# Attention, experts and a gated FFN on one core: routing tables filled during the first pair of heads, one copy issued later, output scales computed beside the experts, the last queries of two heads normalized together

## The chip, the cores and the metric

The kernel runs on one core of one Trainium2 chip. The core has five engines with a program each: TensorE (PE, matmul and transpose; its weight loads stand as PEld), VectorE (DVE), ScalarE (ACT), GpSimd (POOL) and SyncE (SP, which here issues nearly all DMAs). Each works its instructions off in the order in which they were issued and meets the others only at semaphores. The metric is the device time of one execution in microseconds (us); smaller is better.

## The reference

Three stages follow one another.

1. Attention, for 4 batches of 8 heads, 1152 keys, head width 64. Queries are averaged in twos, so 576 queries are left per head: `attn = softmax(q_pool @ k.T / 8)`, `out = attn @ v`. The heads of a batch side by side are the rows `x` (2304 tokens of 512).
2. A mixture of 8 experts with one expert per token: `logits = x @ w_gate`, the expert is the largest logit, its softmax probability the weight: `out[mask] = gate_w * (relu(x[mask] @ w1[e]) @ w2[e])`.
3. A gated FFN: `(x @ w_a) * (x @ w_b) @ w_out`, with the three matrices given in float64.

## The kernel before

**Tiling of the attention.** The 32 heads are worked in 16 pairs (`NPAIR`), two neighbouring heads at a time. Values are held as a high and a low float16 part, so that a product takes up to three matmuls. Of the 576 queries of a head, 512 are four full blocks of 128; the last 64 of both heads share a fifth block: queries 512 to 575 of head 0 in rows 0 to 63, those of head 1 in rows 64 to 127. `spread(p)` (L312, ACT) makes two copies per pair, one in `qq` and one in `qlt`: it puts the last columns of each head in a block by itself, with zeros beside it, for the row maxima of the fifth block.

**Two passes over the scores.** The first finds each query's maximum: `a_units` (L319) issues matmuls into PSUM tile `sa` (two buffers) for two (block, third of the keys) parts, and DVE takes the maximum (`mx`, L338). `finish_max` (L343) turns the maxima into two more rows of the query side (`rl`, by a DMA transpose). The second pass goes in 21 units per pair, `n` counted over all 336: `scores(n)` (L370, PSUM tile `sp`, two buffers), two exponentials on ACT (`pt` in float32, L387, and `ph` in float16, L389), `p_low` (L404), which on POOL subtracts them (`pl`, L407), and four units later (`LAG`) `av(n)` (L409), which multiplies `ph` and `pl` with the values.

**The order of the work** is written out by hand in the loop over `n` (L960 to L1064), and that order holds on every engine. `a_ends` (L929) spreads the first pass of a pair over units of the pair before: the rest of pair 0 goes to units 0 to 5, all of pair 1 to units 6 to 15. Table `U` (L955) gives the unit `u` of a pair at which the other work is issued: for pair p+2 the splitting and transposing of keys (`prep_k`, `prep_k_low`, `trans_k`) and queries (`prep_q`, `prep_q_low`, `trans_q1`, `spread`), loads for pair p+3, and the finishing of pair p-1: `norm(p-1, 1)` at u = 4, `norm_tail` at 6, `turn` (transposes on TensorE, then ACT) at 7 and 10, `turn_low` at 9 and 11, `mag_x` at 12, `logits` at 13. For pair 1 there is no pair before to hide in, so its first preparations come at n = 0 and 1: at n = 1 `trans_k(1)`, `prep_q_low(1)`, `trans_q1(1)` and `spread(1)`, whose two ACT copies read what the two DMA transposes of `trans_q1(1)` write.

**`norm_tail(p)`** (L468) divides the fifth block by its sums. It does head 0 with three DVE instructions on rows 0 to 63 and head 1 with three on rows 64 to 127, whose result goes to tile `xtl`; a DMA then moves it to rows 0 to 63, beside head 0, in `xe`. In the last pair both heads' last queries lie in rows 0 to 63 and no DMA is needed.

**Routing.** After the fourth pair of a batch, generators (`scales`, `gate`, `out_scale`) are appended to `gates`, and `aside()` takes one step of them in every second unit. `out_scale(b)` (L614) makes the factor by which a token's row is multiplied at the very end: five small DVE instructions (a sum over `gex`, the exponentials of the logits, plus 1e-9, a reciprocal, times `am`, the row's scale, and a product), in two steps. For batches 0 to 2 it runs in the attention, for batch 3 after `route()` (L1091). `places()` (L1220) runs beside the experts, two steps per slot of 64 tokens, and uses the factor `osc` at L1264.

**Start.** Before the first load is used, POOL writes the identity (`ident`), index tables (`iota_*`, `koff`, `tok_base`) and `upper`, and DVE the tables `desc`, `tri`, `pad_id`, `out_id` and `upper16`, and shifts `iota_row2` and `tok_base`. All are for the transposes of `turn` and for the routing; the DVE instructions that depend on POOL's tables (L137 to L143, L218) stand in DVE's program ahead of, in the order in which they ran, the low parts of pair 0's keys (L272). The matmuls `warm` (L886) only keep TensorE busy.

Of the kernel before, what the change touches and what calls it, by code (L numbers as in the profile page):

```python
# [27 lines left out]
def attn_moe_kernel(  # L28
# [58 lines left out]
    ident = cst.tile([128, 128], F32, name="ident")  # L87
    make_identity(nc, ident)
    ones_col = cst.tile([128, 1], F32, name="ones_col")
# [4 lines left out]
    nc.vector.memset(ones16, 1.0)  # L94


    desc, desc_ = [cst.tile([128, NTB, E], F32, name=f"desc{i}") for i in range(2)]
    for i, d in enumerate((desc, desc_)):
        for e in range(E):
            nc.vector.memset(d[:, :, e : e + 1], float(E - e))  # L100
        nc.vector.memset(d[64:128, NTB - 1, :], -float(i))

    tri = cst.tile([128, E, E], F32, name="tri")
    nc.vector.memset(tri, 0.0)
    for e in range(1, E):
        nc.vector.memset(tri[:, e, 0:e], 1.0)
    iota_row = cst.tile([128, 128], F32, name="iota_row")
    nc.gpsimd.iota(iota_row, pattern=[[1, 128]], base=0, channel_multiplier=0, allow_small_or_imprecise_dtypes=True)

    iota_row2 = cst.tile([128, 2, TS], F32, name="iota_row2")  # L110
    nc.gpsimd.iota(iota_row2, pattern=[[0, 2], [1, TS]], base=0, channel_multiplier=0, allow_small_or_imprecise_dtypes=True)

    iota_slot = cst.tile([128, 2, NP], F32, name="iota_slot")
    nc.gpsimd.iota(
        iota_slot, pattern=[[1, 2], [2, NP]], base=0, channel_multiplier=0, allow_small_or_imprecise_dtypes=True
    )
    iota_tile = cst.tile([128, NT // 128], F32, name="iota_tile")
    nc.gpsimd.iota(
        iota_tile, pattern=[[1, NT // 128]], base=0, channel_multiplier=0, allow_small_or_imprecise_dtypes=True
    )  # L120
    iota_part = cst.tile([128, 1], F32, name="iota_part")
    nc.gpsimd.iota(iota_part, pattern=[[0, 1]], base=0, channel_multiplier=1, allow_small_or_imprecise_dtypes=True)

    koff = cst.tile([128, 3, E], F32, name="koff")
    nc.gpsimd.iota(koff, pattern=[[1, 3], [0, E]], base=0, channel_multiplier=0, allow_small_or_imprecise_dtypes=True)
    iota_e = cst.tile([128, E], F32, name="iota_e")
    nc.gpsimd.iota(iota_e, pattern=[[1, E]], base=0, channel_multiplier=0, allow_small_or_imprecise_dtypes=True)

    tok_base = cst.tile([128, B, NTB], F32, name="tok_base")
    for i in range(2):  # L130
        nc.gpsimd.iota(
            tok_base[:, 2 * i : 2 * i + 2], pattern=[[SQ, 2], [128, NTB]], base=i * 128 - PAD * (1 - i),
            channel_multiplier=1, allow_small_or_imprecise_dtypes=True,
        )

    pad_id = cst.tile([128, 1], F32, name="pad_id")
    nc.vector.tensor_scalar(out=pad_id, in0=iota_part, scalar1=float(TS), scalar2=-float(TS), op0=ALU.is_ge, op1=ALU.mult)  # L137
    nc.vector.tensor_tensor(out=pad_id, in0=pad_id, in1=iota_part, op=ALU.add)
    nc.vector.tensor_scalar(out=pad_id, in0=pad_id, scalar1=float(PAD), scalar2=None, op0=ALU.add)
    for t in (iota_row2, tok_base):  # L140
        nc.vector.tensor_scalar(out=t, in0=t, scalar1=R_OFF, scalar2=None, op0=ALU.subtract)
    out_id = cst.tile([128, 1], F32, name="out_id")
    nc.vector.tensor_scalar(out=out_id, in0=iota_part, scalar1=float(PAD), scalar2=None, op0=ALU.add)  # L143
    lpx = cst.tile([128, 9, 1], F32, name="lpx")
# [59 lines left out]
    for i in range(3):  # L204
# [7 lines left out]
    upper = at.tile([128, 128], F32, name="upper")  # L212
    nc.gpsimd.memset(upper, 1.0)
    nc.gpsimd.affine_select(
        out=upper, in_=upper, compare_op=ALU.is_gt, fill=0.0, base=0, pattern=[[1, 128]], channel_multiplier=-1
    )
    upper16 = at.tile([128, 128], F16, name="upper16")
    nc.vector.tensor_copy(upper16, upper)  # L218

# [228 lines left out]

    xtl = at.tile([128, D], F32, name="xtl")


# [16 lines left out]
    def norm_tail(p):  # L468
        b, h = bh(p)
        x = xe[b][0:64, 4, 64 * h : 64 * h + 128]  # L470
        for j in range(2):
            o = tail(p, j)
            ps = slice(o.base_partition(), o.base_partition() + 64)
            r = rec[ps, 4 + j]
            nc.vector.tensor_scalar(out=r, in0=o[:, D : D + 1], scalar1=VC * PX * 1e-9, scalar2=None, op0=ALU.add)
            nc.vector.reciprocal(r, r)
            y = xtl[64:128] if ps.start else x[:, D * j : D * j + D]
            nc.vector.tensor_scalar(out=y, in0=o[:, 0:D], scalar1=r, scalar2=None, op0=ALU.mult)
            if ps.start:
                nc.sync.dma_start(out=x[:, D : 2 * D], in_=y)  # L480

# [44 lines left out]

    p2 = {}


    def scales(b):  # L530
        am = p2[b] = ap2.tile([128, NTB, 1], F32, tag="am", name=f"am{b}")
# [12 lines left out]

    gsum = {}

    def gate(b):
# [5 lines left out]
        yield  # L553
        ex = gsum[b] = ap2.tile([128, NTB, E], F32, tag="gex", name=f"gex{b}")
        nc.scalar.activation(ex, sh, AF.Exp)
        o = oh[:, b]
# [53 lines left out]
        )  # L610
        yield


    def out_scale(b):  # L614
        gs = ap2.tile([128, NTB, 1], F32, tag="gs", name=f"gs{b}")
        nc.vector.tensor_reduce(out=gs, in_=gsum[b], axis=AX.X, op=ALU.add)
        nc.vector.tensor_scalar(out=gs, in0=gs, scalar1=1e-9, scalar2=None, op0=ALU.add)
        yield
        nc.vector.reciprocal(gs, gs)
        nc.vector.tensor_tensor(out=gs, in0=gs, in1=p2[b], op=ALU.mult)  # L620
        nc.vector.scalar_tensor_tensor(out=osc[:, b], in0=gs, scalar=OS, in1=gs, op0=ALU.mult, op1=ALU.mult)
        yield
# [251 lines left out]
    with tc.manual_schedule():  # L874
# [85 lines left out]
        for n in range(NPAIR * NU):  # L960
# [64 lines left out]
            if p:  # L1025
                if u == U["n1"]:
                    norm(p - 1, 1)
                if u == U["nt"]:
                    norm_tail(p - 1)
                if u in U["t"]:  # L1030
                    turn(p - 1, [0, 1, 2, 3] if u == U["t"][0] else [4])
                if u in U["tl"]:
                    turn_low(p - 1)
                if u == U["mg"]:
                    mag_x(p - 1)
                if u == U["lg"]:
                    logits(p - 1)
                if p % HP == HP - 1 and u == U["sx"]:
                    store_x(p // HP, 0, HP - 1)
                if p % HP == 0 and u == U["g"]:  # L1040
                    gates.extend(x(p // HP - 1) for x in (scales, gate, out_scale))
            for _ in range(ASIDE[u] if n > 9 else 0):
# [46 lines left out]
        for _ in routing:  # L1089
            pass  # L1090
        gates.append(out_scale(B - 1))  # L1091
        while gates:
            aside()
    at_ctx.close()
# [125 lines left out]
    def places():  # L1220
# [38 lines left out]
        yield  # L1259

        bv = mp.tile([128, NB, 2, NO], F32, name="obv")
        nc.vector.tensor_tensor(out=bv[:, :, 0], in0=bm, in1=vf.to_broadcast([128, NB, NO]), op=ALU.mult)
        yield
        nc.vector.tensor_tensor(  # L1264
            out=bv[:, :, 1], in0=bm, in1=osc.rearrange("p b i o -> p (b i) o").to_broadcast([128, NB, NO]), op=ALU.mult
        )
# [206 lines left out]
```

## Time and profile before

| | |
|---|---|
| three runs | 1302.93, 1309.43, 1310.91 us (median 1309.43) |
| profiled execution | 1305.76 us; its span in the trace 1304.1 us |
| PE busy | 1181.3 us (91% of the span), 17154 matmuls |
| DVE busy | 798.9 us (61%), 1546 instructions |
| ACT busy | 648.2 us (50%), 1325 |
| POOL busy | 525.3 us (40%), 471 |
| mean granted TensorE clock | 0.963 |
| pass over the scores and routing (attention) | 0 to about 565 us |
| experts | about 567 to 861 us |
| gated FFN | about 866 us to the end |

How to read it: the span counts from the first instruction of the trace. Busy shares are means over three stages with different limits, so every reading that follows is of a stretch. In a row of a timeline the bracket at the end, `[5.10 <-ACT ph L389]`, says that the engine stood idle for 5.10 us just before that instruction, and that what it waited for last was ACT's instruction at line 389, which writes `ph`. The granted clock is a share of TensorE's full speed, 2.4 GHz; 0.50 is the lower of its two levels, 1.2 GHz.

### The profile page before, as it was taken

To read this page: it belongs to the slowest core of one execution; us is meant where nothing else is said; L and a number is where in the kernel's file an instruction comes from. 1 tells how busy PE (TensorE), PEld (TensorE's weight loads), DVE (VectorE), ACT (ScalarE), POOL (GpSimd) and SP (SyncE) were. 2 spreads that over 40 slices of the span, in tenths; PEclk is the share of its full clock that TensorE was granted. 3 is DMA by queue.
4 is the path that set the end of the run, shared out by engine and by line. 5 is a ranking of instruction groups with operands and counts; after the bars stand their busy time and mean duration, and the time that the engine had idled before them with its cause. 6 is when DMAs were issued, how large, how long until landed. Compare 5 with 4: busy or idle time off the path is not lost. (4 is left out here: it accounts for less than half of the span.)

```text
span 1304.1 us, 41111 instructions
## 1 busy us (share of the span) xinstructions
PE 1181.3 (91%) x17154; PEld 823.2 (63%) x17154; DVE 798.9 (61%) x1546; ACT 648.2 (50%) x1325; POOL 525.3 (40%) x471
## 2 busy tenths in 40 slices
PE   7799999899889998578978998989999999999996
PEld 6466665566556655378878997964555555555553
DVE  5678788778878887855485557238577722222221
ACT  3578887788778877522473336225443311111111
POOL 4578887788878877613243322100000000000000
PEclk9899999999999999778989998999999999999998
DMA  7666775566646533244187227113222100000000
GB/s 173 121 136 152 147 180 148 106 139 142 121 93 156 121 74 108 71 168 156 48 315 260 89 78 253 49 31 104 81 83 96 33 1 1 25 25 25 25 17 33
DMA packets 170508, 136.46 MB, mean 105 GB/s; under 512 B 101072, under 2 KB 136400, under 8 KB 170256
## 3 DMA queue, kind: packets, MB, share of 16 engines
q1 hardware_dynamic: 167056, 122.74, 35.4%
q0 software_dynamic: 3200, 10.53, 2.4%
q8 instruction: 136, 2.23, 0.7%
q14 instruction: 116, 0.95, 0.2%
HBM read 94.96 MB, written 9.74 MB: 80 GB/s over the span
## 5 line engine op out<-in xcount | busy, mean ns | idle before, releaser
L407 POOL TENSOR_TENSOR pl<-pt,ph 128x512 f16<-128x512 f32 (+1 forms) x330 | 383.3, 1178 | 112.5 <-ACT ph L389 82.8
L387 ACT ACTIVATE pt<-sp 128x512 f32<-128x512 f32 (+1 forms) x336 | 197.5, 588 | 103.9 <-PE sp L380 96.4
L338 DVE TENSOR_REDUCE mx<-sa 128x2 f32<-128x768 f32 x224 | 206.2, 923 | 70.2 <-PE sa L333 67.5
L1383 PEld LDWEIGHTS <-wc 128*128 128x128 f16 x1728 | 169.5, 98 | 125.0 <-PEq L1345 4.7
L1383 PE MATMUL ab<-x2h,wc 128*128 128x384 f16 x1152 | 212.0, 327 | 4.6 <-PEq L1345 4.6
L429 PEld LDWEIGHTS <-ph 128*128 128x128 f16 (+1 forms) x2880 | 151.3, 101 | 75.8 <-issue 35.5
L1422 POOL DMA_INDIRECT out_dram<-ob,idxo x18 | 17.5, 973 | 444.6 <-DVE ob L1421 411.7
L389 ACT ACTIVATE ph<-sp 128x512 f16<-128x512 f32 (+1 forms) x331 | 195.1, 590 | 0.0
L333 PE MATMUL sa<-kst,qq 128*128 128x384 f16 x480 | 159.1, 332 | 29.1 <-DVE mx L338 25.3
L429 PE MATMUL av<-vv,ph 128*128 128x65 f16 (+2 forms) x2880 | 168.9, 196 | 0.3 <-DVE ph L402 0.3
L1393 DVE TENSOR_TENSOR gf<-ab,sa 128x384 f32<-128x384 f32 x72 | 40.1, 557 | 194.5 <-PE ab L1383 194.4
L333 PE MATMUL sa<-kst,qlt 128*128 128x384 f16 x480 | 158.7, 331 | 0.0
L429 PE MATMUL av<-vv,pl 128*128 128x65 f16 (+1 forms) x1440 | 156.4, 194 | 1.0 <-POOL pl L407 1.0
L1182 PEld LDWEIGHTS <-w2c 128*128 128x128 f16 x3840 | 128.5, 102 | 28.7 <-issue 21.6
L380 PE MATMUL sp<-rl,k2b 66*128 66x512 f16 (+1 forms) x576 | 136.8, 292 | 8.0 <-DMA rl<-qln 7.1
L377 PE MATMUL sp<-qq,kst 128*128 128x512 f16 (+1 forms) x576 | 136.0, 290 | 7.3 <-ACT ph L389 7.2
L1161 PE MATMUL hp<-xh,w1c 128*128 128x64 f16 x2560 | 125.1, 194 | 6.1 <-issue 1.4
L1161 PEld LDWEIGHTS <-w1c 128*128 128x128 f16 x3840 | 120.3, 99 | 10.3 <-DVE w1c L866 5.4
L429 PEld LDWEIGHTS <-pl 128*128 128x128 f16 (+1 forms) x1440 | 123.8, 102 | 1.2 <-POOL pl L407 1.1
L1182 PE MATMUL yp<-hh,w2c 128*128 128x64 f16 x2560 | 114.0, 199 | 8.3 <-issue 3.6
L1161 PE MATMUL hp<-xl,w1c 128*128 128x64 f16 x1280 | 121.4, 194 | 0.0
L1383 PE MATMUL ab<-x2l,wc 128*128 128x384 f16 x576 | 117.3, 326 | 0.0
(230 smaller groups left out, 1825.0 us busy)
## 6 DMA issues: line engine op xcount, KB each, us to landing
raw<-in_moe_w_dram SPq DMA_DIRECT2D x20, 1024.0 KB, 6.9
rbw<-in_moe_w_dram SPq DMA_DIRECT2D x20, 1024.0 KB, 7.4
kr<-in_k_dram SPq DMA_DIRECT2D x16, 576.0 KB, 5.2
vr<-in_v_dram SPq DMA_DIRECT2D x16, 576.0 KB, 6.1
qr<-in_q_dram SPq DMA_DIRECT2D x32, 256.0 KB, 3.5
cl<-in_moe_w_a_dram SPq DMA_DIRECT2D x12, 512.0 KB, 3.5
cl<-in_moe_w_b_dram SPq DMA_DIRECT2D x12, 512.0 KB, 3.7
cl<-in_moe_w_out_dram SPq DMA_DIRECT2D x12, 512.0 KB, 3.4
```

The source lines that it names most:

```text
L333: nc.tensor.matmul(sa[:, i, :KA], lhsT=x[:, 128 * b_ : 128 * b_ + 128], rhs=kst[:, j, ks], start=o == 0, stop=o == len(ops) - 1,)
L338: nc.vector.tensor_reduce(out=s["mx"].rearrange("p t n -> p (t n)")[:, ones[0] : ones[0] + m].rearrange("p (m o) -> p m o", o=1), in_=sa[: ...
L377: nc.tensor.matmul(sp[:, o : o + w], lhsT=s["kst"][:, j, ks], rhs=s["qq"][:, c0 : c0 + w], start=True, stop=False)
L380: nc.tensor.matmul(sp[:, o : o + w], lhsT=k2b[p % 3][:, j, ks], rhs=s["rl", j if w > 64 else 1][0:66, c0 : c0 + w], start=False, stop=True,)
L387: nc.scalar.activation(pt[:, :o], sp[:, :o], AF.Exp, scale=1.0 / (16.0 * SC * SC))
L389: nc.scalar.activation(phb[n % NPB][0][:, :o], sp[:, :o], AF.Exp, scale=1.0 / (16.0 * SC * SC))
L407: eng.tensor_tensor(out=l[:, :w], in0=pts.pop(n)[:, :w], in1=h[:, :w], op=ALU.subtract)
L429: nc.tensor.matmul(o, lhsT=a, rhs=b_, start=first, stop=False, skip_group_check=True)
L1161: nc.tensor.matmul(hp[:, j], lhsT=wc[:, t, i], rhs=g[x][:, i, w], start=first, stop=(j == 3 and i == KD - 1 and x == "xl"), skip_group_che ...
L1182: nc.tensor.matmul(y[:, d], lhsT=wc[:, t, 128 * d : 128 * d + 128], rhs=hs[s, n][x][:, j], start=first, stop=(n == 1 and len(terms) == 1 a ...
L1383: nc.tensor.matmul(ps[:, 0:TB], lhsT=w_[:, t, m, 128 * i : 128 * i + 128], rhs=x_[:, i, ts_], start=(i + j == 0), stop=(j == 2 and i == KD ...
L1393: nc.vector.tensor_tensor(out=gf, in0=pair[1], in1=sa, op=ALU.mult)
```

## The change

- The tables of the start are not written at the start. A list `late` of 16 functions holds them, all for POOL (the memsets, the arithmetic and the cast that DVE did are POOL's as well now), and units 5 to 20 of the first pair take one function each. In all these are 46 POOL instructions (identity 2, `desc` 18, `tri` 8, index tables 9, ids 4, offsets 2, `upper` 3).
- `spread(1)` is issued at n = 8, not n = 1.
- `out_scale` is gone. `gex` and `p2` keep the exponentials and row scales of all batches, and `places()` computes `osc` for all 20 blocks in the same five DVE instructions, in two more steps.
- `norm_tail` normalizes rows 0 to 127 at once, with three DVE instructions in `xe` itself, and the DMA moves head 1's part from rows 64 to 127 to rows 0 to 63. The last pair keeps its two sets.
- In the last pair the finishing of pair 14 is spread further: `turn` of the fifth block at u = 13 (10 before), `turn_low` of it at 14 (11), `mag_x` at 15 (12), `logits` at 15 (13).

```diff
-    make_identity(nc, ident)
+    late = [lambda: make_identity(nc, ident)]
...
+    def fill_desc(i):
+        d = (desc, desc_)[i]
         for e in range(E):
-            nc.vector.memset(d[:, :, e : e + 1], float(E - e))
-        nc.vector.memset(d[64:128, NTB - 1, :], -float(i))
+            nc.gpsimd.memset(d[:, :, e : e + 1], float(E - e))
+        nc.gpsimd.memset(d[64:128, NTB - 1, :], -float(i))
+
+    late += [lambda: fill_desc(0), lambda: fill_desc(1)]
...
-    nc.vector.tensor_scalar(out=out_id, in0=iota_part, scalar1=float(PAD), scalar2=None, op0=ALU.add)
+
+    def fill_ids():
+        G = nc.gpsimd
...
+    def fill_off():
+        for t in (iota_row2, tok_base):
+            nc.gpsimd.tensor_scalar(out=t, in0=t, scalar1=R_OFF, scalar2=None, op0=ALU.subtract)
+
+    late += [fill_ids, fill_off]
...
-    nc.vector.tensor_copy(upper16, upper)
+
+    def fill_upper():
...
+        nc.gpsimd.tensor_copy(upper16, upper)
+
+    late.append(fill_upper)
...
     def norm_tail(p):
         b, h = bh(p)
-        x = xe[b][0:64, 4, 64 * h : 64 * h + 128]
-        for j in range(2):
-            o = tail(p, j)
-            ps = slice(o.base_partition(), o.base_partition() + 64)
+        x = xe[b][:, 4, 64 * h : 64 * h + 128]
+        last = p == NPAIR - 1
+        for j in range(1 + last):
+            ps = slice(0, 64 if last else 128)
+            o = tail(p, j) if last else st[p]["o", 1][:, 4 * (D + 1) : 5 * (D + 1)]
             r = rec[ps, 4 + j]
             nc.vector.tensor_scalar(out=r, in0=o[:, D : D + 1], scalar1=VC * PX * 1e-9, scalar2=None, op0=ALU.add)
             nc.vector.reciprocal(r, r)
-            y = xtl[64:128] if ps.start else x[:, D * j : D * j + D]
-            nc.vector.tensor_scalar(out=y, in0=o[:, 0:D], scalar1=r, scalar2=None, op0=ALU.mult)
-            if ps.start:
-                nc.sync.dma_start(out=x[:, D : 2 * D], in_=y)
+            nc.vector.tensor_scalar(out=x[ps, D * j : D * j + D], in0=o[:, 0:D], scalar1=r, scalar2=None, op0=ALU.mult)
+        if not last:
+            nc.sync.dma_start(out=x[0:64, D:], in_=x[64:128, 0:D])
...
+            if n == 8:
                 spread(1)
+            if 5 <= n and late:
+                late.pop(0)()
...
+                ut, utl, ulg = [(U["t"], U["tl"], U["lg"]), ([7, 13], [9, 14], 15)][not nxt]
...
-                    gates.extend(x(p // HP - 1) for x in (scales, gate, out_scale))
+                    gates.extend(x(p // HP - 1) for x in (scales, gate))
...
-        gates.append(out_scale(B - 1))
-        while gates:
-            aside()
     at_ctx.close()
...
+        gs = mp.tile([128, NB, 1], F32, name="ogs")
+        osc = mp.tile([128, NB, 1], F32, name="osc")
+        nc.vector.tensor_reduce(out=gs, in_=gex.rearrange("p b i e -> p (b i) e"), axis=AX.X, op=ALU.add)
+        nc.vector.tensor_scalar(out=gs, in0=gs, scalar1=1e-9, scalar2=None, op0=ALU.add)
+        yield
+        nc.vector.reciprocal(gs, gs)
+        nc.vector.tensor_tensor(out=gs, in0=gs, in1=p2.rearrange("p b i o -> p (b i) o"), op=ALU.mult)
+        nc.vector.scalar_tensor_tensor(out=osc, in0=gs, scalar=OS, in1=gs, op0=ALU.mult, op1=ALU.mult)
+        yield
```

## Rows read from the trace of the kernel before

**Rows 1.** Busy time by stretch: PE, PEld, DVE, ACT, POOL, then clock, DMA share, GB/s

```profile
55.00:70.00 15.00, 14.08 (x166) 9.11 (x165) 13.54 (x21) 10.12 (x22) 9.61 (x10) 1.00 0.78 169
...
270.00:370.00 100.00, 90.02 (x1328) 59.90 (x1327) 85.42 (x164) 79.71 (x164) 84.72 (x74) 1.00 0.59 127
...
570.00:640.00 70.00, 64.51 (x1949) 63.09 (x1947) 32.30 (x72) 22.65 (x51) 14.87 (x15) 0.94 0.41 142
```

**Rows 2.** Timeline of the first pair (start us, duration us, engine, line, instruction, wait)

```profile
32.51 0.59 ACT L389 ACTIVATE ph<-sp 128x512 f16<-128x512 f32 x1
...
42.09 0.30 ACT L314 COPY qlt<-qlt 128x128 f16<-128x128 f16 x1 [1.15 <-DMA qlt<-qln]
...
43.42 0.58 PE L377 MATMUL sp<-qq,kst 128*128 128x512 f16 x1 [5.10 <-ACT ph L389]
...
48.97 0.51 PE L333 MATMUL sa<-kst,qq 128*128 128x384 f16 x1
```

**Rows 3.** Timeline, TensorE from 140 to 500 us: five waits for DVE

```profile
147.06 0.32 PE L333 MATMUL sa<-kst,qq 128*128 128x384 f16 x1 [0.82 <-DVE mx L338]
...
208.28 0.32 PE L333 MATMUL sa<-kst,qq 128*128 128x384 f16 x1 [1.23 <-DVE mx L338]
...
243.60 0.32 PE L333 MATMUL sa<-kst,qq 128*128 128x384 f16 x1 [3.55 <-DVE mx L338]
...
369.75 0.32 PE L333 MATMUL sa<-kst,qq 128*128 128x384 f16 x1 [3.56 <-DVE mx L338]
...
494.72 0.32 PE L333 MATMUL sa<-kst,qq 128*128 128x384 f16 x1 [2.73 <-DVE mx L338]
```

**Rows 4.** Timeline, DVE just before the wait that ends at 243.60 us

```profile
237.44 0.67 DVE L617 TENSOR_SCALAR gs<-gs 128x5 f32<-128x5 f32 x1
...
239.55 0.16 DVE L475 TENSOR_SCALAR rec<-av 64x1 f32<-64x1 f32 x1
...
240.26 0.19 DVE L619 RECIPROCAL gs<-gs 128x5 f32<-128x5 f32 x1
240.49 0.96 DVE L620 TENSOR_TENSOR gs<-gs,am 128x5 f32<-128x5 f32 x1
...
242.58 0.96 DVE L338 TENSOR_REDUCE mx<-sa 128x2 f32<-128x768 f32 x1
```

**Rows 5.** Busy time of TensorE by stretch (then clock, DMA share, GB/s), after that wait

```profile
243.60:246.00 2.40, 2.40 (x19) 0.62 0.00 0
246.00:249.00 3.00, 3.00 (x34) 0.74 0.74 137
```

**Rows 6.** Timeline of the last pair, TensorE and ACT

```profile
526.60 0.30 PE L490 MATMUL tp<-ident,xe 128*128 128x128 f32 x1 [2.76 <-DMA xe<-xtl]
...
526.94 0.28 ACT L493 ACTIVATE axh<-tp 128x128 f16<-128x128 f32 x1 [2.03 <-PE tp L490]
```

**Rows 7.** Timeline of the start: DVE, SP's queue and TensorE

```profile
8.69 1.36 DVE L141 TENSOR_SCALAR iota_row<-iota_row 128x128 f32<-128x128 f32 x1
...
9.61 1.31 SPq L293 DMA_TRANSPOSE qlt<-qln  x1
...
10.31 1.79 DVE L272 SCALAR_TENSOR_TENSOR kn<-kr,kn 128x576 f16<-128x576 f32 x2
...
12.15 2.73 SPq L293 DMA_TRANSPOSE kst<-kn  x2
...
15.47 0.48 PE L333 MATMUL sa<-kst,qq 128*128 128x384 f16 x1 [3.86 <-DMA kst<-kn]
```

**Rows 8.** Groups of POOL instructions: shapes, count, busy us, mean ns, idle before

```profile
L407 POOL TENSOR_TENSOR pl<-pt,ph 128x512 f16<-128x512 f32 x282 | 336.6, 1209 | 108.3 <-ACT ph L389 82.0 <-issue 5.7 <-PE av L429 5.6
...
L601 POOL TENSOR_SCALAR amat<-iota_row,row 128x128 f16<-128x128 f32 x3 | 2.0, 672 | 3.8 <-DVE row L596 3.8
...
L108 POOL IOTA iota_row<- 128x128 f32 x1 | 0.2, 244 | 0.0
...
L1457 POOL MEMSET const-float32-1.0<- 128x1 f32 x1 | 0.1, 98 | 0.0
```

More of the change, by code (lines that the diff above doesn't have):

```diff
@@ L94, in attn_moe_kernel @@
     nc.vector.memset(ones16, 1.0)
+    late = [lambda: make_identity(nc, ident)]
     desc, desc_ = [cst.tile([128, NTB, E], F32, name=f"desc{i}") for i in range(2)]
-    for i, d in enumerate((desc, desc_)):
+    def fill_desc(i):
+        d = (desc, desc_)[i]
         for e in range(E):
-            nc.vector.memset(d[:, :, e : e + 1], float(E - e))
-        nc.vector.memset(d[64:128, NTB - 1, :], -float(i))
+            nc.gpsimd.memset(d[:, :, e : e + 1], float(E - e))
+        nc.gpsimd.memset(d[64:128, NTB - 1, :], -float(i))
@@ L103, in attn_moe_kernel @@
+    late += [lambda: fill_desc(0), lambda: fill_desc(1)]
     tri = cst.tile([128, E, E], F32, name="tri")
[L104 to L127, printed above, removed]
+    def fill_tri():
+        nc.gpsimd.memset(tri, 0.0)
+        for e in range(1, E):
+            nc.gpsimd.memset(tri[:, e, 0:e], 1.0)
+    late.append(fill_tri)
@@ new lines, in iota @@
+    def iota(shape, name, pattern, base=0, mult=0):
+        t = cst.tile(shape, F32, name=name)
+        late.append(
+            lambda: nc.gpsimd.iota(
+                t, pattern=pattern, base=base, channel_multiplier=mult, allow_small_or_imprecise_dtypes=True
+            )
+        )
+        return t
+    iota_row = iota([128, 128], "iota_row", [[1, 128]])
+    iota_row2 = iota([128, 2, TS], "iota_row2", [[0, 2], [1, TS]])
+    iota_slot = iota([128, 2, NP], "iota_slot", [[1, 2], [2, NP]])
@@ L129, in attn_moe_kernel, with fill_tok @@
+    iota_tile = iota([128, NT // 128], "iota_tile", [[1, NT // 128]])
+    iota_part = iota([128, 1], "iota_part", [[0, 1]], mult=1)
+    koff = iota([128, 3, E], "koff", [[1, 3], [0, E]])
+    iota_e = iota([128, E], "iota_e", [[1, E]])
     tok_base = cst.tile([128, B, NTB], F32, name="tok_base")
-    for i in range(2):
+    def fill_tok(i):
         nc.gpsimd.iota(
@@ L134, in attn_moe_kernel @@
         )
+    late += [lambda: fill_tok(0), lambda: fill_tok(1)]
     pad_id = cst.tile([128, 1], F32, name="pad_id")
[L137 to L141, printed above, removed]
-    out_id = cst.tile([128, 1], F32, name="out_id")
-    nc.vector.tensor_scalar(out=out_id, in0=iota_part, scalar1=float(PAD), scalar2=None, op0=ALU.add)
+    out_id = cst.tile([128, 1], F32, name="out_id")
+    def fill_ids():
+        G = nc.gpsimd
+        G.tensor_scalar(out=pad_id, in0=iota_part, scalar1=float(TS), scalar2=-float(TS), op0=ALU.is_ge, op1=ALU.mult)
+        G.tensor_tensor(out=pad_id, in0=pad_id, in1=iota_part, op=ALU.add)
+        G.tensor_scalar(out=pad_id, in0=pad_id, scalar1=float(PAD), scalar2=None, op0=ALU.add)
+        G.tensor_scalar(out=out_id, in0=iota_part, scalar1=float(PAD), scalar2=None, op0=ALU.add)
+    def fill_off():
+        for t in (iota_row2, tok_base):
+            nc.gpsimd.tensor_scalar(out=t, in0=t, scalar1=R_OFF, scalar2=None, op0=ALU.subtract)
+    late += [fill_ids, fill_off]
     lpx = cst.tile([128, 9, 1], F32, name="lpx")
@@ L159, in attn_moe_kernel @@
     amat = rt.tile([128, B, NTB, 128], F16, name="amat")
-    osc = rt.tile([128, B, NTB, 1], F32, name="osc")
+    gex = rt.tile([128, B, NTB, E], F32, name="gex")
+    p2 = rt.tile([128, B, NTB, 1], F32, name="p2")
     NP0 = 3
@@ L212, in attn_moe_kernel @@
     upper = at.tile([128, 128], F32, name="upper")
[L213 to L216, printed above, removed]
     upper16 = at.tile([128, 128], F16, name="upper16")
-    nc.vector.tensor_copy(upper16, upper)
+    def fill_upper():
+        nc.gpsimd.memset(upper, 1.0)
+        nc.gpsimd.affine_select(
+            out=upper, in_=upper, compare_op=ALU.is_gt, fill=0.0, base=0, pattern=[[1, 128]], channel_multiplier=-1
+        )
+        nc.gpsimd.tensor_copy(upper16, upper)
+    late.append(fill_upper)
     phb = [[at.tile([128, 512], F16, name=f"p{x}{i}") for x in "hl"] for i in range(NPB)]
@@ L447, in mag_x @@
         )
-    xtl = at.tile([128, D], F32, name="xtl")
     def norm(p, j):
@@ L525, in store_x @@
         nc.sync.dma_start(out=xbuf[r0 + 512 : r0 + SQ, c], in_=x[0:64, n4, c])
-    p2 = {}
     def scales(b):
-        am = p2[b] = ap2.tile([128, NTB, 1], F32, tag="am", name=f"am{b}")
+        am = p2[:, b]
         nc.vector.tensor_reduce(out=am, in_=amx[:, b % 2], axis=AX.X, op=ALU.max)
@@ L543, in scales @@
         yield
-    gsum = {}
     def gate(b):
@@ L553, in gate @@
         yield
-        ex = gsum[b] = ap2.tile([128, NTB, E], F32, tag="gex", name=f"gex{b}")
-        nc.scalar.activation(ex, sh, AF.Exp)
+        nc.scalar.activation(gex[:, b], sh, AF.Exp)
         o = oh[:, b]
@@ L610, in gate @@
         )
[L611 to L621, printed above, removed]
         yield
@@ L1029, in attn_moe_kernel @@
                     norm_tail(p - 1)
-                if u in U["t"]:
-                    turn(p - 1, [0, 1, 2, 3] if u == U["t"][0] else [4])
-                if u in U["tl"]:
+                ut, utl, ulg = [(U["t"], U["tl"], U["lg"]), ([7, 13], [9, 14], 15)][not nxt]
+                if u in ut:
+                    turn(p - 1, [0, 1, 2, 3] if u == ut[0] else [4])
+                if u in utl:
                     turn_low(p - 1)
-                if u == U["mg"]:
+                if u == (U["mg"] if nxt else 15):
                     mag_x(p - 1)
-                if u == U["lg"]:
+                if u == ulg:
                     logits(p - 1)
@@ L1264, in places @@
         nc.vector.tensor_tensor(
-            out=bv[:, :, 1], in0=bm, in1=osc.rearrange("p b i o -> p (b i) o").to_broadcast([128, NB, NO]), op=ALU.mult
+            out=bv[:, :, 1], in0=bm, in1=osc.to_broadcast([128, NB, NO]), op=ALU.mult
         )
```

## The prediction, made before the changed kernel was built or run

> **What bounds the kernel now.** Start with busy time by stretch. In the middle of the attention TensorE is busy 90 us of 100, DVE 85, POOL 85, ACT 80 [rows 1]: TensorE leads, and its idle time there is what can be won. The next view is TensorE's timeline, read for idle time above 0.3 us and what ended it. In the attention there are three kinds.
>
> First, a hole in the first pair [rows 2]. ACT's last exponential ahead of it starts at 32.51 and lasts 0.59 us; then ACT stands until the two copies of spread(1), the second of which waits for the DMA transpose of qlt and starts at 42.09. ACT works in order, so unit 3's exponentials wait behind it, both sp buffers stay full, and TensorE idles 5.10 us until 43.42. After that its matmul of 512 columns takes 0.58 us; at 48.97 one of 384 takes 0.51, against 0.32 in the middle of the attention [rows 3]: the clock is at its lower level.
>
> Second, waits for DVE at units 7 and 8 of a pair [rows 3]. The row of 147.06 stands for six pairs (0.81 to 0.82 us each), that of 208.28 for three (1.23 each); three others have 3.55, 3.56 and 2.73. In those three DVE's timeline [rows 4] shows in front of the late maximum the two steps of out_scale (from 237.44 and from 240.26) and the two tail sets; the second set takes 240.26 - 239.55 = 0.71 us.
>
> Third, 2.76 us in the last pair for the DMA of head 1's last queries, which leaves ACT idle for 2.03 us [rows 6].
>
> **The change, part by part.** The sum is made against the profiled execution, 1305.8 us; the median of the runs shown is 3.7 us above it.
>
> Spread(1) at n = 8. Behind it in ACT's queue stood the exponentials of units 3 and 4, whose scores lay ready, and two key splits of pair 2. Next late are the transposes of pair 1 themselves: unit 6 issues the first maxima of pair 1, which read qlt, so TensorE cannot pass there before about 42.09. Can it be there by then? It stopped at 43.42 - 5.10 = 38.32; the work from 43.42 to 48.97, 5.55 us at mostly the lower clock, should take half, so 41.1. Unit 6 then starts at 42.1 instead of 48.97: 6.9 us, and 0.1 for the slow matmuls still to come. **7.0 us**; ends 5.1 (that work as slow as before, 38.32 + 5.55 = 43.9) and 7.4. The copies at n = 8 delay nobody: they are needed for the fifth block of pair 1, at unit 15. The maxima of pair 0's second head come earlier with unit 5, and with them their transpose, so the second head's scores are not the next wait.
>
> Tables out of the start [rows 7]. DVE's L141 and the instructions behind it lie between 8.69 and 10.31 ahead of the low keys; these end at 10.31 + 1.79 = 12.10, and the transposes of kst go out at 12.15. SP is free from 9.61 + 1.31 = 10.92. With the tables gone the transposes go out there, all loads queued behind them on SP too, and the first maxima at 15.47 come as much earlier: **1.2 us**. Ends 0 (the low keys still wait) and 1.8 (with a shorter wait than 3.86 us the clock may hold).
>
> The same tables on POOL in units 5 to 20 [rows 8]: 9 index tables of at most 0.24, 28 memsets of about 0.1, nine others between 0.1 and 0.67: about 2 + 3 + 3 = 8 us. The cover is POOL's idle time, 5.4 us of 15 [rows 1]; over 16 units of some 1.45 us (two maxima, scores, av) it is 8.3. Behind a table on POOL wait only subtractions, which av uses four units later. **0 us** on the path; to +5.5 if every table instruction takes 0.3 (46 x 0.3 - 8.3). Without that cover they would cost their 8 us.
>
> Three tail instructions fewer [rows 4]. The trace has no set on 128 rows; I take it as long as one on 64, since the columns are the same, and 0.1 off for safety: 0.6 of the 0.71. In the six pairs with 0.82 and the three with 1.23, TensorE is what waits: 9 x 0.6 = **5.4 us**; ends 0 and 6.4. In pairs 1, 2 and 15 nothing. The DMA remains one per pair, with the same bytes, and starts earlier.
>
> Out_scale out of the attention. In the three pairs the maximum at 242.58 would come about 0.8 (first step) + 2.3 (240.26 to 242.58) + 0.7 (tail set) = 3.8 us earlier; the waits become like those of the six pairs after their gain. 3.55 + 3.56 + 2.73 = 9.84, less 3 x 0.25: **9.1 us**; ends 4.5 (half) and 9.8. The clock comes with it: after 243.60 it is granted at 0.62 and 0.74 [rows 5], which costs 0.38 x 2.4 + 0.26 x 3.0 = 1.7 us of TensorE; the equally long wait before 369.75 counts the same. As other engines limit part of it I take 1.3 each, **2.6 us**; ends 0 and 3.4.
>
> The same five instructions beside the experts, four times as wide, once: each is between the 0.19 of L619 and the 1.07 that an L621 took. DVE is busy 32 of 70 us there and TensorE 64.5 [rows 1], so it is mostly hidden: **+0.5 us**, ends 0 and +3. One of the small ones shows why they can be dear: L620 takes 0.96 us on five columns [rows 4], beside POOL's subtractions.
>
> [...]
>
> The last pair. At u = 13 the DMA has three more units to land; of the 2.76 us ACT felt 2.03 [rows 6], and ACT, with two exponentials per unit and the expert weights to split, leads there. **1.5 us**; ends 0 and 2.8.
>
> Sum: 7.0 + 1.2 + 5.4 + 9.1 + 2.6 + 1.5 - 0.5 = 26.3 us, so 1305.8 - 26.3 = 1279.5. As that execution lies below the median of its kernel I add half of the 3.7: **1281 us**.
>
> **The rivals.**
>
> A, the middle fills up again. When DVE no longer stops TensorE, POOL, busy 84.7 of 100 us [rows 1], does: its subtractions come late and TensorE waits at av or ACT for a free pt. Then 5.4, 9.1 and 2.6 are lost: 1305.8 - 9.2 = 1296.6, or 1298 with the 1.9 added. For it: POOL's share. Against it: the waits that end come just before spots where POOL has four units of slack, and a pair shortened by 0.6 to 3.5 us of some 29.5 raises POOL's share by 2 to 10 points only in those pairs.
>
> B, the change does not do what it says at the start: the hole stays, because pair 1's transposes and not the copies hold everything. Then 7.0 and 1.2 are lost: 1305.8 - 18.1 + 1.9 = 1289.6. Against it: 38.32 to 42.09 is only 3.8 us of the 10.65 from 38.32 to 48.97.
>
> C, slower: a small POOL instruction costs as much as a subtraction, 1.21 us [rows 8]. Then 46 x 1.21 = 55.7 us, less 8.3 of cover, keep the subtractions and with them av late in the first pair: 47.4 - 26.8 = +20.6, so 1326 or 1328. It decides from (26.3 + 8.3) / 46 = 0.75 us each. For it: no POOL arithmetic below 0.67 us is in the trace. Against it: memsets and index tables, 37 of the 46, show 0.1 to 0.24.
>
> **The numbers.** Forecast 0.70, A 0.18, B 0.08, C 0.04. A measurement of this kernel tells changes from about 1% on, 13 us, that is below 1296.3. Forecast and B are faster by more (0.78), of A a small part: faster 0.79; A otherwise and a poor forecast: same 0.17; C: slower 0.04. Range: the good ends of the terms sum to 31.6, 1274, and 4 us for the spread of the runs below: 1270. Above it reaches over A with its spread: 1301; what is left out is C and the far ends.
>
> **What would show it.** In the trace after: ACT without a wait for a DMA between 33 and 42 us, and TensorE's first maxima of pair 1 near 41, at full clock (if they start at 44 or later, the first term is wrong). The kst transposes near 11 us. Waits for DVE at units 7 and 8 of 0.3 us or less in pairs 3 to 14, no clock loss after pairs 6 and 10, and no new waits for POOL in their place (A). POOL in units 5 to 20 with subtractions at most two units behind ACT (C). No wait for xe's DMA in the last pair. Wrong would be above all a middle whose pairs still take as long with the waits gone.

## The result and the profile after

The changed kernel took 1293.47 us (median of 4 runs, 1285.94 to 1293.95), the kernel before 1309.55: ratio 0.9878, 95% interval 0.9842 to 0.9914. Six later runs, beside new ones of the kernel before, gave 0.9896 (0.9868 to 0.9925). So the gain is 14 to 16 us where 26 were forecast. In the profiled executions it is 1305.8 - 1293.2 = 12.6 us. The first expert matmul stands at 559.16 us against 566.66, so 7.5 us of that were won in the attention and the routing; the other 5.1 lie behind, where the fourteen profiled executions told of here take anything from 728.3 to 737.4 us, so they can't be put down to the change.

**The start and the first pair** [rows 2, 7]. Timeline of the changed kernel, then of the groups of POOL's instructions (by shape: count, busy us, mean ns, idle before).

```profile
10.79 2.86 SPq L316 DMA_TRANSPOSE kst<-kn  x2
...
34.02 1.67 DVE L309 SCALAR_TENSOR_TENSOR qln<-qs,qn 128x576 f16<-128x576 f32 x1
...
36.62 0.48 PE L356 MATMUL sa<-kst,qq 128*128 128x384 f16 x1 [3.17 <-DVE mx L361]
...
39.64 0.60 ACT L410 ACTIVATE pt<-sp 128x512 f32<-128x512 f32 x1 [5.02 <-PE sp L403]
...
42.07 0.33 PE L356 MATMUL sa<-kst,qq 128*128 128x384 f16 x1
...
44.87 0.60 ACT L410 ACTIVATE pt<-sp 128x512 f32<-128x512 f32 x1 [0.37 <-PE sp L403]
...
46.80 0.38 PE L403 MATMUL sp<-rl,k2b 66*128 66x512 f16 x1 [0.80 <-DMA rl<-qln]
...
48.25 0.30 ACT L337 COPY qq<-qq 128x128 f16<-128x128 f16 x1
```
```profile
L159 POOL TENSOR_SCALAR iota_row<-iota_row 128x128 f32<-128x128 f32 x1 | 1.1, 1056 | 0.1
L103 POOL MEMSET desc<- 128x5 f32 x16 | 0.7, 103 | 0.0
...
L154 POOL TENSOR_SCALAR pad_id<-pad_id 128x1 f32<-128x1 f32 x1 | 0.2, 233 | 0.1
```

The transposes of kst go out at 10.79, 1.36 us earlier. ACT no longer stands for a transpose; the exponentials of unit 8 start at 44.87 against 52.08. The hole is not gone, though: ACT now stands 5.02 us for scores, because TensorE waits 3.17 us for a maximum queued on DVE behind the qln of 1.67 us (`qn` is the high part of the queries, which DVE copies to a second place, L308; `qln` is their low part, which DVE computes, L309). The tables on POOL are as cheap as predicted.

**The middle** [rows 3, 4]. Timeline of the changed kernel, pair 3: DVE, POOL, and TensorE with what ended its waits; then the same TensorE row in other pairs.

```profile
138.64 8.40 POOL L430 TENSOR_TENSOR pl<-pt,ph 128x512 f16<-128x512 f32 x7
...
142.00 1.33 DVE L308 COPY qn<-qn 128x576 f16<-128x576 f16 x1
...
143.25 1.67 DVE L309 SCALAR_TENSOR_TENSOR qln<-qs,qn 128x576 f16<-128x576 f32 x1
...
144.86 0.67 DVE L519 SCALAR_TENSOR_TENSOR axl<-tp,axh 128x512 f16<-128x512 f32 x1
...
145.59 0.38 PE L511 MATMUL tp<-ident,xe 128*128 128x128 f32 x1 [1.81 <-DVE axl L519]
...
178.23 0.33 PE L511 MATMUL tp<-ident,xe 128*128 128x128 f32 x1 [1.82 <-DVE axl L519]
...
240.19 0.33 PE L511 MATMUL tp<-ident,xe 128*128 128x128 f32 x1 [1.82 <-DVE axl L519]
...
428.99 0.46 PE L511 MATMUL tp<-ident,xe 128*128 128x128 f32 x1 [1.83 <-DVE axl L519]
```

The waits for the maxima at units 7 and 8 of 0.82 and 3.55 us are gone. At unit 10 a new one stands in eight pairs, 1.81 to 1.83 us each: the transpose of the last queries (`tp`) needs a buffer of the maxima's scores (`sa`) that axl frees (the low part of the turned outputs, `turn_low`), and axl stands on DVE behind the copy and the qln of the next queries (unit 9). In the kernel before, these two took 0.43 and 0.73 us:

```profile
144.65 4.50 POOL L407 TENSOR_TENSOR pl<-pt,ph 128x512 f16<-128x512 f32 x4
...
148.90 0.43 DVE L285 COPY qn<-qn 128x576 f16<-128x576 f16 x1
149.25 0.73 DVE L286 SCALAR_TENSOR_TENSOR qln<-qs,qn 128x576 f16<-128x576 f32 x1
...
149.92 3.38 POOL L407 TENSOR_TENSOR pl<-pt,ph 128x512 f16<-128x512 f32 x3 [0.78 <-ACT ph L389]
```

There POOL had run out of work at 149.15 and stood 0.78 us; TensorE's stop of 0.82 at unit 7 had held ACT's exponentials back. But for their first 0.25 us, the copy and the qln ran in that pause. Take the stop away, and POOL's subtractions run back to back (8.40 us for seven).

The trace of before held an example of that. In pairs 1 and 2 TensorE has no wait above 0.25 us at units 7 and 8, POOL's subtractions run back to back, the qln takes 1.68 and 1.67 us, and the transpose at unit 10 waits 1.32 and 1.54 us for axl. Pair 2 of the kernel before:

```profile
117.81 0.94 DVE L285 COPY qn<-qn 128x576 f16<-128x576 f16 x1
118.67 1.67 DVE L286 SCALAR_TENSOR_TENSOR qln<-qs,qn 128x576 f16<-128x576 f32 x1
...
121.02 0.33 PE L490 MATMUL tp<-ident,xe 128*128 128x128 f32 x1 [1.54 <-DVE axl L498]
```

The clock adds to it [rows 5]. Busy time by stretch behind the wait of 145.59 (PE, PEld, DVE, ACT, POOL, clock, DMA share, GB/s):

```profile
146.00:148.00 2.00, 2.00 (x27) 1.45 (x25) 0.60 (x2) 0.70 (x2) 1.04 (x1) 0.50 0.92 174
148.00:150.00 2.00, 2.00 (x22) 1.11 (x20) 0.62 (x1) 0.78 (x3) 1.16 (x1) 0.71 0.78 220
```

0.50 is the lower level, 1.2 GHz, reached after 1.81 us in which TensorE stood. It does not follow every such wait: behind that of 178.23 the clock stays at 1.00. From one such wait to the next, with the lower clock behind the first and without (same columns):

```profile
145.59:178.23 32.64, 29.91 (x422) 19.83 (x422) 24.29 (x39) 24.99 (x51) 25.71 (x23) 0.95 0.70 170
272.69:302.96 30.27, 28.30 (x423) 18.92 (x424) 24.30 (x39) 24.99 (x51) 25.48 (x23) 1.00 0.66 149
```

TensorE is busy 1.6 us longer in the first for the same work: that is the clock's part. Most of the rest is a wait of 0.90 us for `rl` at 161.63. In the kernel before such a pair took 29.32 us (274.90 to 304.22), so the new wait costs about 1 us where the clock stays up, and 1.6 more where it falls.

Added up by pair, each from its first exponential on ACT to that of the next pair, the 7.5 us won by the first expert matmul come together like this. Up to the second pair 5.9 us are won (74.80 against 68.94). The six ordinary pairs 3, 4, 7, 8, 11 and 12 (those of 0.82 in rows 3) lose 8.7 us (176.8 before, 185.5 after). Pairs 6, 10 and 14, which had the three long waits, win 6.8 (99.2 and 92.4), pairs 5, 9 and 13 win 2.9, the rest 0.7.

**The last pair** [rows 6]. Timeline, TensorE and, in front of its second wait, DVE:

```profile
519.86 0.33 PE L511 MATMUL tp<-ident,xe 128*128 128x128 f32 x1 [0.28 <-DMA xe<-xe]
...
523.33 1.38 DVE L425 CAST ph<-pt 128x512 f16<-128x512 f32 x1
524.63 0.81 DVE L467 TENSOR_REDUCE amx<-xe 128x5 f32<-128x640 f32 x1
...
526.20 1.41 DVE L871 SCALAR_TENSOR_TENSOR w1c<-raw,w1c 128x512 f16<-128x512 f32 x1
...
528.79 0.47 PE L511 MATMUL tp<-ident,xe 128*128 128x128 f32 x1 [2.74 <-DVE xe L499]
```

The wait for the DMA fell from 2.76 to 0.28 us. The pair's own last queries are late instead, by 2.74 us: what was moved to unit 15 stands in DVE's queue ahead of them.

### The profile page after: what moved, and what is told of

Its sections match the earlier page's. It is cut to its first block, busy times and chain, and to the rows that moved or that the text cites. A ratio compares the mean times of both kernels' runs of the same rounds, so it can differ in the third digit from the quotient of the medians.

```text
span 1291.5 us, 41065 instructions
## 1 busy us (share of the span) xinstructions
PE 1176.2 (91%) x17154; PEld 819.1 (63%) x17154; DVE 790.5 (61%) x1453; ACT 649.9 (50%) x1325; POOL 538.0 (42%) x504
## 5 line engine op out<-in xcount | busy, mean ns | idle before, releaser
L430 POOL TENSOR_TENSOR pl<-pt,ph 128x512 f16<-128x512 f32 (+1 forms) x330 | 388.6, 1197 | 92.3 <-ACT ph L412 70.6
```

The lines of the kernel that those rows point to most:

```text
L430: eng.tensor_tensor(out=l[:, :w], in0=pts.pop(n)[:, :w], in1=h[:, :w], op=ALU.subtract)
```

## The experiments

Ratios are to the kernel before on the same chip, with 95% intervals; 0.01 is 13 us.

**e1_tail**: the kernel before, with the last queries of both heads in one set.
```diff
-        for j in range(2):
-            o = tail(p, j)
+        for j in range(1 + last):
+            o = tail(p, j) if last else st[p]["o", 1][:, 4 * (D + 1) : 5 * (D + 1)]
```


> The kernel before with one edit: the last queries of both heads in one set of three instructions. Theory (a wait took the place of the one removed): TensorE's waits for the maxima at units 7 and 8 shrink by 0.6 to 0.8 us, but without that stop POOL stays behind with its subtractions, DVE's low parts of the next queries (the copy and qln) run beside them at about 1.3 and 1.7 us instead of 0.43 and 0.73, and the transpose of the last queries at unit 10 waits 1.8 us in the six ordinary pairs: 6 x (+1.0) and 6 x (-0.7), so +2 us, between -2 and +5 of the time before, with the 1.8 us waits in the trace. Rival (the term of 5.4 us holds and the loss is elsewhere): 5 us faster, and no new wait at unit 10.

Measured: 0.9977 (0.9958 to 0.9995), 3.0 us faster (0.7 to 5.5). The time lies between the two, and the trace shows the theory's mechanism: copy and qln average 0.98 and 1.49 us (0.38 and 0.93 before; here and below means of ten pairs, 140 to 440 us), and the new wait is there.

```profile
151.91 0.37 PE L489 MATMUL tp<-ident,xe 128*128 128x128 f32 x1 [1.81 <-DVE axl L497]
```

The 3.0 us rest on the medians alone. The profiled execution (1310.38 us) lies 4.5 above its median and reaches the first expert matmul 6.9 us later than that of before: four of its six ordinary pairs have the lower clock (0.95 on the mean) and take 31.8 to 32.9 us.

**e2_osc**: the kernel before, with the output scales beside the experts.
```diff
-                    gates.extend(x(p // HP - 1) for x in (scales, gate, out_scale))
+                    gates.extend(x(p // HP - 1) for x in (scales, gate))
...
+        nc.vector.tensor_reduce(out=gs, in_=gex.rearrange("p b i e -> p (b i) e"), axis=AX.X, op=ALU.add)
```


> The kernel before with one edit: the output scales computed beside the experts. Theory: the three waits of 3.55, 3.56 and 2.73 us become like those of the ordinary pairs, about 0.8, because the tail sets are still there and POOL still gets its pause: 7 to 11 us faster, copy and qln at 0.43 and 0.73 us in the ordinary pairs. Rival (out_scale was hardly worth anything, as in the changed kernel, where these pairs still wait 1.8 us): 3 to 5 us faster.

Measured: 0.9851 (0.9829 to 0.9873), 19.5 us faster: this one part is worth at least about as much as the whole change (0.9878 and 0.9896). Theory and rival were both too low. The three long waits became 0.82, 0.81 us and none, copy and qln stayed at 0.40 and 0.93 us, and the clock from 76 to 500 us rose from 0.98 to 1.00.

```profile
239.59 0.32 PE L334 MATMUL sa<-kst,qq 128*128 128x384 f16 x1 [0.82 <-DVE mx L339]
```

By the first expert matmul (552.74) 13.9 us are won in the profiled executions. Pairs 6, 10 and 14, which had the three long waits, are together 11.0 us shorter (99.2 before, 88.2 here). Pairs 5 and 13 are 3.3 us shorter, all of it at a clock of 1.00 where the profile of before has 0.95; e3_spread, with out_scale in place, has 1.00 there too, so this need not be out_scale's. Of the 19.5 the two profiled executions show 15.4; that of before lies 3.2 us below the 1308.9 that the kernel before took beside this one.

**e3_spread**: the kernel before, with spread(1) at n = 8.
```diff
-                spread(1)
+            if n == 8:
+                spread(1)
```


> The kernel before with one edit: the second pair's spread copy at n = 8. Both theories: the hole of 5.10 us before 43.42 us goes. If what is won there is kept, 7 us faster; if part of it is given back in units 13 to 21 to waits for DVE and for the scores, as the trace of the changed kernel suggests, 5 to 6 us faster at the start of the second pair and at the end.

Measured: 0.9967 (0.9951 to 0.9983), 4.3 us. From the first exponential to the second pair's first it takes 40.55 us (31.00 to 71.55), against 44.95 before (29.85 to 74.80) and 40.60 in the changed kernel (28.34 to 68.94). What is late next here is the second pair's transposes, as the prediction said, but at 44.55 and not at 42.09:

```profile
43.53 0.34 PE L333 MATMUL sa<-kst,qq 128*128 128x384 f16 x1 [1.15 <-DMA qq<-qn]
44.55 0.34 PE L333 MATMUL sa<-kst,qlt 128*128 128x384 f16 x1 [0.69 <-DMA qlt<-qln]
```

**e4_low_first**: the changed kernel, with axl issued ahead of copy and qln.
```diff
                 if v_ == U["ql"]:
+                    if p:
+                        turn_low(p - 1)
                     prep_q_low(p + 2)
...
-                if u in utl:
+                if u in utl and not (u == U["ql"] and p + 2 < NPAIR):
```


> The changed kernel with one edit: at unit 9 the low part of the turned outputs is issued ahead of the next queries' copy and qln. Theory: the wait of 1.8 us of the transpose at unit 10 goes in the eight pairs that show it, as DVE has freed its buffer before the slow copy and qln begin; the maximum behind them comes 0.7 us later, which eats part: 8 to 14 us faster than the changed kernel. Rival (POOL or ACT limits these pairs anyway): 0 to 3 us faster, with TensorE waiting elsewhere as long.

Measured: 0.9793 (0.9763 to 0.9823), 27 us below the kernel before and 11 to 13 below the changed one. Copy and qln still average 0.77 and 1.49 us, but from 80 to 470 us nothing waits for axl; the maximum behind them is waited for 0.80 us.

```profile
141.23 0.68 DVE L519 SCALAR_TENSOR_TENSOR axl<-tp,axh 128x512 f16<-128x512 f32 x1
141.82 0.73 DVE L308 COPY qn<-qn 128x576 f16<-128x576 f16 x1
142.48 1.68 DVE L309 SCALAR_TENSOR_TENSOR qln<-qs,qn 128x576 f16<-128x576 f32 x1
...
145.08 0.32 PE L356 MATMUL sa<-kst,qq 128*128 128x384 f16 x1 [0.80 <-DVE mx L361]
```

**e5_two_sets**: the changed kernel, with the two tail sets back.
```diff
-        for j in range(1 + last):
-            o = tail(p, j) if last else st[p]["o", 1][:, 4 * (D + 1) : 5 * (D + 1)]
+        for j in range(2):
+            o = tail(p, j)
```


> The changed kernel with one part undone: the last queries of the two heads in two sets again, as before. Theory (the shorter tail takes POOL's pause away): the waits of 1.8 us at unit 10 go and those of 0.82 us at units 7 and 8 come back, copy and qln take 0.43 and 0.73 us; with what the other parts gave alone (19.5 us for the output scales, 4.3 for the spread copy, 1 to 2 for the tables) 1282 to 1287 us, that is 6 to 11 us faster than the changed kernel. Rival (the tail is a gain of some 3 us by itself, as measured alone, and adds): 1296 us.

Measured: 0.984 (0.9818 to 0.9863). Six instructions instead of three in every pair, and some 5 to 7 us faster than the changed kernel (clear of the noise against its six later runs, not against its first four); the waits of 0.82 us are back and copy and qln average 0.40 and 0.93.

```profile
143.90 0.32 PE L356 MATMUL sa<-kst,qq 128*128 128x384 f16 x1 [0.82 <-DVE mx L361]
...
145.73 0.42 DVE L308 COPY qn<-qn 128x576 f16<-128x576 f16 x1
146.08 0.74 DVE L309 SCALAR_TENSOR_TENSOR qln<-qs,qn 128x576 f16<-128x576 f32 x1
```

**e6_skip**: the changed kernel with fewer subtractions on POOL.
```diff
-            if n:
+            if n and not (0 < p < NPAIR - 1 and u in (5, 6)):
                 p_low(n - 1, l_eng(n - 1))
```


> The changed kernel, leaving out POOL's subtraction for units 4 and 5 of pairs 1 to 14 (the low parts of those probabilities are stale), so that POOL has caught up by unit 9; DVE's order is untouched. Theory: DVE's copy and qln then run at about 0.43 and 0.73 us, the transpose at unit 10 no longer waits 1.8 us, and the time comes to 1276 to 1284 us, like the kernel with the low part issued first. Rival (copy and qln are slow for a reason other than POOL): they stay at 1.3 and 1.7 us, the wait stays, 1290 to 1294 us.

Measured: 0.9761 (0.9745 to 0.9776), 1273.4 us. DVE's order is that of the changed kernel, yet copy and qln average 0.36 and 0.93 us and the waits of 1.8 us are gone from the eight pairs. So POOL is what holds them. Part of the time is the work left out, which can't be separated.

```profile
144.71 1.16 POOL L430 TENSOR_TENSOR pl<-pt,ph 128x512 f16<-128x512 f32 x1 [0.25 <-ACT ph L412]
146.50 4.57 POOL L430 TENSOR_TENSOR pl<-pt,ph 128x512 f16<-128x512 f32 x4 [0.64 <-PE av L452]
```
```profile
145.67 0.37 DVE L308 COPY qn<-qn 128x576 f16<-128x576 f16 x1
145.97 0.73 DVE L309 SCALAR_TENSOR_TENSOR qln<-qs,qn 128x576 f16<-128x576 f32 x1
146.64 0.67 DVE L519 SCALAR_TENSOR_TENSOR axl<-tp,axh 128x512 f16<-128x512 f32 x1
```

**e7_last**: e4_low_first, with the last pair's own transpose one unit later.
```diff
-                if u == (U["mg"] if nxt else 15):
+                if u == (U["mg"] if nxt else 18):
...
-                if u == NC + 5 + LAG:
+                if u == NC + 6 + LAG:
                     turn(p, [4])
...
```


> The kernel with the low part issued first (1280.6 us), with the last pair's own last-query transpose and its low part one unit later and the magnitudes of the pair before it at unit 18. Theory (DVE's queue is what the transpose of 512.40 us waits for, 3.00 us): the wait falls below 1 us and the first expert matmul comes 2 to 3 us earlier, 1278 us. Rival (POOL's and ACT's share of that stretch limits it): the wait moves to an av or a score, 1280 to 1282 us.

Measured: 0.978 (0.9754 to 0.9806), not distinguishable from e4_low_first. The wait fell from 3.00 to 0.94 us, but from the last wait for rl to the first expert matmul it takes 52.39 us (490.22 to 542.61) against 52.48. The rival holds:

```profile
513.21 0.33 PE L511 MATMUL tp<-ident,xe 128*128 128x128 f32 x1 [0.94 <-DVE xe L499]
515.71 0.23 PE L452 MATMUL av<-vv,ph 128*128 128x65 f16 x2 [0.41 <-DVE ph L425]
516.95 0.20 PE L452 MATMUL av<-vv,pl 128*128 128x65 f16 x1 [1.00 <-POOL pl L430]
```

**e8_low_first_two_sets**: the edits of e4_low_first and e5_two_sets together.

> The kernel with the low part issued first (1280.6 us), with the last queries in two sets again, which prices the single set where the wait at unit 10 cannot form. Theory: the single set is worth what the prediction gave it, about 5 us, once nothing takes its place: 1284 to 1287 us. Rival (it is worth nothing in any surrounding): 1279 to 1282 us.

Measured: 0.9848 (0.9832 to 0.9864), 7 us slower than with one set (0.9793 in e4_low_first; 0.978 in e7_last, beside this run). So the shorter tail is worth what the prediction gave it, or a little more, once axl stands ahead.

**e9_tables_back**: the changed kernel, with the tables at the start, on DVE and POOL.
```diff
-            if 5 <= n and late:
-                late.pop(0)()
```


> The changed kernel with one part undone: the routing tables filled at the start again, on DVE and POOL as before. Both views of the start: the first maxima come at 15.4 instead of 14.3 us. The prediction's term: 1.2 us slower than the changed kernel, 1295 us. Rival, from the spread copy alone, which brought the second pair forward by 3.3 us against 5.9 in the changed kernel: the second pair's transposes, behind the same queue, are then what TensorE waits for in the first pair (near 43.5 us), and 2 to 3 us are lost by the start of the second pair, 1296 us.

Measured: 0.9899 (0.988 to 0.9919) against 0.9896 for the changed kernel beside it: no difference in the time. The last wait for rl ahead of the second pair ends at 70.55 us, in two profiles of the changed kernel at 68.47 and 69.17; what the tables win at the start is not found again at the end. In the profiles the clock hides it: from 76 to 500 us it is 0.99 here and 0.98 in both of the changed kernel. No transpose of the second pair is waited for, so the rival's reason falls in this run; in the repeated run of the changed kernel they are waited for (0.69 us until 42.18), about where the prediction set the earliest point.

**e10_q3**: the changed kernel, with POOL's 1.40 us of pooling three units earlier.
```diff
-            ... q=6, ql=9,
+            ... q=3, ql=9,
```


> The changed kernel with one number changed: POOL's pooling of the queries (1.40 us, ahead of the subtractions in its queue) at unit 3 instead of 6. Theory: POOL's lag at unit 9 comes from this add; with three more units to make it up, copy and qln fall to about 0.4 and 0.9 us on the mean, the wait of 1.8 us at unit 10 goes in most pairs, 1278 to 1284 us. Rival: POOL, at 85% busy, has not caught up by unit 9 all the same, copy and qln stay above 0.7 and 1.4 us, and the time stays within 4 us of the changed kernel, 1289 to 1297 us.

Measured: 0.987 (0.984 to 0.9901). Copy and qln average 0.93 and 1.68 us, the wait is 1.56. The rival holds in the trace: POOL does not catch up in six units, and copy and qln stay slow. The time, 1287.75 us, is 2.8 below the changed kernel's beside it, between the rival's and the theory's. So the one instruction is not what keeps POOL behind; that its load as a whole does, 85% busy, fits but is not shown by this run.

```profile
178.75 0.33 PE L511 MATMUL tp<-ident,xe 128*128 128x128 f32 x1 [1.57 <-DVE axl L519]
```

**e11_last_q3**: e7_last with q=3.

> All that helped so far in one kernel: low part first, the last pair's transpose one unit later, and POOL's pooling of the queries at unit 3. Theory: the waits of 0.8 us for the maximum behind the slow copy and qln go too, 14 pairs at up to 0.5 us and the clock with them: 3 to 6 us below the kernel without the last edit, a ratio to before of 0.973 to 0.976. Rival: nothing is left to gain there, a ratio of 0.978.

Measured: 0.9798 (0.9774 to 0.9823). The wait for the maximum fell from 0.81 to 0.56 us, and the time did not follow. The three versions with axl ahead and one tail set (0.978 to 0.9798) are alike, and all beat both kernels; that reorder is what helps.

**e12_after_again**: the changed kernel itself.

> The changed kernel once more, beside the others on one chip, as its result rests on four runs: a ratio to before of 0.984 to 0.991, and in the profile a wait of the transpose at unit 10 of 1.8 us in the same eight pairs.

Measured: 0.9896 (0.9868 to 0.9925), with the waits of 1.80 to 1.82 us in the same eight pairs.

## Why the prediction was half right

**Spread copy, 7.0 us.** Too large. By itself it gave 4.3 us of time, and 4.4 of the 44.95 us up to the second pair (40.55 in e3). In the changed kernel unit 8 comes 7.2 us earlier (44.87 against 52.08), but 1.5 of these are the tables'. Units 8 to 20 give back 1.3, most of it in a wait of 0.80 us for the second head's `rl` (46.80), which the prediction had ruled out ("the second head's scores are not the next wait"). The bound of 42.09 us for the transposes of pair 1 was early too: in six runs that wait for them, they hold TensorE until 42.18 to 44.55. That the first maxima of pair 1 start at 42.07 us, 0.33 us each, the full clock's duration, as forecast, is in part luck: TensorE had waited 3.17 us for DVE on the way.

**Tables, 1.2 us; fills on POOL, 0.** The start came 1.2 to 1.5 us earlier (the first exponentials at 28.34 us, 29.85 before, 29.87 in e9); in the time it does not show. The fills cost 0.1 to 0.3 us each, one 1.06, and rival C falls.

**Three tail instructions fewer, 5.4 us.** This step failed. "In the six pairs with 0.82 and the three with 1.23, TensorE is what waits", it said, and took the end of that wait for a gain. The stop was also POOL's pause, and the pause was where copy and qln ran. Without it they take 1.15 and 1.67 us on the mean (0.38 and 0.93 before), and 1.8 us of wait replace 0.8. The six ordinary pairs were to be 3.6 us shorter together and are 8.7 longer, part of it by the clock. By itself the part gained 3.0 us, in the changed kernel it costs 5 to 7 (e5), and with axl moved it gives 7 (e4 against e8). The rows that could have warned were those of pairs 1 and 2, where the prediction saw "nothing" to win and did not ask why they had no stop, a slow qln and a wait at unit 10.

**Out_scale, 9.1 and 2.6 us.** The mechanism was right: in e2 the three pairs are 11.0 us shorter, where these two terms make 11.7. The time of that run shows more, 19.5 us (16.6 to 22.4), with two tail sets still in place. In the changed kernel two of these three pairs fall into the new wait (240.19, 366.88), with the clock at 0.95 again, so that 6.8 us of it were left; "no clock loss after pairs 6 and 10" did not come.

**Scales beside the experts, 0.5 us.** Right: five instructions of 0.18 to 0.31 us at 607.3 us, for which nobody waits. The prediction had seen what POOL does to a small DVE instruction (L620, 0.96 us on five columns "beside POOL's subtractions"), but used it only here.

**Last pair, 1.5 us.** From the wait for rl to the first expert matmul it gained 0.5 us in these two profiles (511.67 to 566.66 before, 504.70 to 559.16 after), but 1.4 in the repeated run (506.54 to 560.12). Four executions without this part take 55.0 to 55.8 us, six with it 53.3 to 54.5, so the size was about right. The DMA's wait became one for DVE, and e7 shows that behind that one stand POOL's subtractions.

**The rivals.** A had the right place and the wrong engine. It said that POOL's results would come late; what came late were DVE's instructions beside POOL. From its time (1298) the measured one is 4.5 us away, from the forecast's (1281) 12.5; the range holds it because it was drawn to reach over A. (C's sum takes off 26.8 where the terms make 26.3; that changes nothing.) It is luck that the three parts measured alone add up to 26.8 us, the size of the forecast: by these times spread copy and tail were each some 2.5 too large, out_scale 7.8 too small.

**The hold.** The traces show it directly. POOL's subtractions beside the copy and the qln of pair 3 in the changed kernel, one by one:

```profile
141.99 1.15 POOL L430 TENSOR_TENSOR pl<-pt,ph 128x512 f16<-128x512 f32 x1
143.10 1.20 POOL L430 TENSOR_TENSOR pl<-pt,ph 128x512 f16<-128x512 f32 x1
144.27 1.66 POOL L430 TENSOR_TENSOR pl<-pt,ph 128x512 f16<-128x512 f32 x1
```

The copy starts just behind the first of them (142.00) and ends 0.18 us after it; the qln starts in the second (143.25) and ends 0.61 us after it. This repeats: from 80 to 470 us, in the kernels before and after, all 18 qln that start while a subtraction runs end 0.61 or 0.62 us after that subtraction, and 16 of 19 such copies 0.18 or 0.19 us after it. With POOL idle the qln takes 0.73 or 0.74 us and the copy 0.32. It works the other way too: the subtraction that starts while the qln is at work takes 1.66 us, not 1.15. The maxima on DVE stay at 0.95 us in both kernels. The Trainium skill ("SBUF — State Buffer", section "Who interferes with whom") says that whichever of DVE and GpSimd issues first keeps the ports that they share to SBUF, the on-chip memory where qn and qln lie, for its whole instruction, that a copy and an instruction with two SBUF inputs can be exposed to it, and a reduction is not. The trace agrees on all three.

Open is what makes the clock fall behind some waits of 1.8 us and not behind others, and how much of e2's 19.5 us beyond the 11.0 of its three pairs is out_scale's.

## What to carry to other kernels

Before a short wait is removed, look at what other engines do while it lasts: a pause that an engine off the critical path enjoys may be where a sensitive instruction of another engine runs. A gain that was measured for a part alone does not add up (3.0 + 19.5 + 4.3 us alone, 14 to 16 together), so test the change with each part undone as well. Where DVE and POOL share a stretch, issue what the bottleneck waits for ahead of the instructions that POOL can hold.

## What was not expected of the hardware

A DVE copy of 128x576 in f16 takes 0.32 us while POOL stands and up to 1.35 beside its subtractions, by how much of a subtraction is left when it starts; the qln takes 0.73 and 1.67. In an ordinary pair the two so cost 1.8 us more than before, on an engine that the table of busy times shows no fuller (346.7 us of 424 against 348.6 from 76 to 500 us), since other work had been taken from it.
